# Broadcasting the tap weights over 128 rows of a cleared tile, with five constant matmuls ahead of it

## The chip, the cores and the metric

The kernel runs on one core of one Trainium2 chip. The time is the device time of one execution in microseconds (us). A core has a matrix engine (TensorE, PE in the profile, with its weight loads as PEld), a vector engine (VectorE, DVE), an activation engine (ScalarE, ACT), a general engine (GpSimd, POOL) and a queue engine (SyncE, SP). Loads and stores are DMA transfers, issued from the SP, ACT and POOL queues. Matmuls write to PSUM, from which ACT and VectorE bring the results to SBUF.

## The reference

The inputs are a sequence of 2048 tokens of width 640 and its weights, all bf16. Cut to what matters:

```python
h  = x + q_ln * (longconv(kv, ssm_k) + kv * ssm_D)   # q_ln = layernorm(x)
#   kv = (4-tap causal convolution of k along the sequence, with shift_k[d, 0..3]) * v
#   longconv: causal convolution over all 2048 tokens, by FFT in the reference
h2 = h + (silu(ln(h) @ w_gate) * (ln(h) @ w_up)) @ w_down   # inner width 1728
```

The tap weights `A_shift_k` (640 channels by 4 taps) are what the change concerns. Nothing of what is computed changes.

## The kernel before, in words

The sequence is cut into four blocks of 512 tokens (i = 0..3), and the long filter into four blocks as well (m = 0..3). Each block of kv and of the filter is taken by matmuls with tables of cosines and sines into 256 complex frequencies (`xf` and `kf`), the blocks are multiplied there (`p`), the sums are taken back by matmuls (`iv`), and the result goes through the second layer norm (`iv..m`, `s`, `v`, `r`, `n`) and a transposing load (`ht`) into the feed-forward part: `fg` (gate) and `fu` (up) matmuls, `sg`, `su` and `sv` on ACT, `mu` on VectorE, and `dn` (down), after which `rs` and `ra` add the residual and `out` stores. The order of the blocks is the string `SEQ`.

**Tasks and the plan.** Each step is a task, added with `g.add` under a name, with what it reads and writes. From this the class `_Graph` finds which task waits for which (`add`). The order on each engine is written out: `PLAN` holds for PE, ACT, DVE, POOL and SP a list of task numbers, and `arrange` takes them as they stand. `PLAN["units"]` says in which of four PSUM units each PSUM tile lies; a PE task that opens a tile waits for the readers of the tile that had the unit before. `emit` writes the waits and the instructions. An engine works strictly in its list's order, so a waiting task holds back all behind it. Since numbers are places in the order of `g.add`, one new task renumbers all after it.

**Fillers.** `PLAN["fills"]` names PE tasks ahead of which `filler` (L499) issues a number of matmuls of 128x512 on a tile of ones (`zmem`, a part of `gu`, set by POOL). They write into the PSUM tile that the task is about to open and their result is not used. Before, there are three ahead of `wb0` and one ahead of `k0t4.0`.

**The opening.** These are the tasks that the change touches, with their lines:

- `ident` and `wrow` (L466 and L469): loads of constants and of the tap weights. `wrow` is a tile of 5x64x4 elements by row. Of its rows only two are filled: row r holds the weights of channels 64r to 64r+63 of each of the five chunks of 128 channels. It goes out on the ACT queue; the other loads of the opening go out on SP.
- `wb0`, `wb4` (line L510): five matmuls that spread the two rows over the 128 partitions. The stationary operand `halfrow` (part of the constants `idall`) is 1 in row 0 for columns 0 to 63 and in row 1 for columns 64 to 127, else 0; the moving operand is one chunk of `wrow`, 256 columns. `wb0` has four chunks, `wb4` the last.
- `diag0`, `diag4` (L516): VectorE multiplies the spread weights with an identity, so that each tap is a diagonal 64x64 matrix per half of the partitions. All taps of all blocks use them.
- `k0t...` (L528): 20 transposes of the first block of K, and `k0e` (L455 on ACT, L457 on DVE): the copies into `kT0`.
- `tp0.4`, `tp0.2`, `tp0.0` (L731): the taps of block 0, 70 matmuls with 64 rows, two at a time in the two halves of the array.
- `kv0.c` (L749): VectorE multiplies the five chunks of the tap sums with v, out of PSUM.
- `kt0` (L547): transposes of the filter's block 0; `xf0` (L599): the forward transform of block 0; `la0` (L827 and after): the moments of x for the first layer norm.

Both operands of the broadcast are two rows high:

```python
last = e.matmul(pt.f(b // 2, 256, o=256 * (b % 2)), halfrow, wrow[0:2, c0 + b].rearrange("p x u -> p u x"), start=True, stop=True)
```

Of the kernel before, what the change touches and what calls it, by code (L numbers as in the profile page):

```python
# [12 lines left out]
P = 128  # L13
# [37 lines left out]
class _Graph:  # L51


    def __init__(self, nc, es):
        self.nc = nc
        self.es = es
        self.tasks = []
        self.tilelist = []
        self.lastw = {}
        self.readers = {}  # L60
        self.fills = PLAN.get("fills", {})
        self.ps = es.enter_context(nc.psum_tensor("ps", [P, 4096], dt.float32))
        self.psb = self.ps[:].bitcast(dt.bfloat16)
# [70 lines left out]
    def arrange(self, plan):  # L134
# [14 lines left out]
        byname = {t.name: t for t in self.tasks}  # L149
        for name, fill in self.fills.items():  # L150
            byname[name].deps.add(byname[fill[0]])
# [28 lines left out]
    def emit(self, block):  # L180
# [85 lines left out]
    "act":  # L266
# [10 lines left out]
    "dve":  # L277
# [10 lines left out]
    "pool":  # L288
        "19 17 15 16 125 165 174 158 192 183 223 225 224 342 396 362 281 371 285 401 380 289 406 389 343 293 420 415 527 466 "
        "470 561 474 552 478 579 570 684 586 591 529 705 710 698 637 732 723 641 645 750 649 741 "  # L290
        "",
    "sp":
        "0 2 3 8 4 6 10 7 230 9 11 13 14 235 296 226 12 229 297 227 481 231 167 176 228 234 295 233 194 185 482 232 364 282 373 "
# [5 lines left out]
        "01310112312301210312031012210230131023033303012010313012013"  # L299
        "",  # L300
    "fills": {
        "wb0": ["zmem", 3],
        "k0t4.0": ["zmem", 1],
    },
}
# [920 lines left out]
```

## Time and profile before

| what | us |
|---|---|
| median of the runs (258.29 to 261.71, three) | 258.99 |
| the profiled execution | 259.3 |
| its span, first to last instruction | 257.3 |
| PE busy | 249.3 |
| DVE busy | 200.0 |
| ACT busy | 184.5 |
| POOL busy | 58.5 |

The profile comes from one execution, and its times count from the start of the span. The 2.0 us between span and time lie around the program. In a timeline row stand the start, the duration, the engine, the line, the operation with the tile that it writes and those that it reads, how many were merged into the row, and in brackets the idle time of the engine before it and what ended it. Matmuls are pipelined: the duration of one is longer than the distance to the next. Buffer numbers are left out of the names, so that `kT` can be `kT0`, and `v` is `v0`. In a row of the windows stand the stretch, its length, then for PE and PEld the busy time and in brackets the number of instructions, then the granted TensorE clock, the DMA share and GB/s.

### The profile page before, as it was taken

What the parts mean: (1) busy time and instruction counts of PE and PEld (TensorE: products, weight loads), DVE (VectorE), ACT (ScalarE), POOL (GpSimd) and SP (SyncE); (2) the same over time, 40 slices, a digit from 0 to 9 for tenths busy, and PEclk for the clock granted to TensorE, in tenths of its full rate; (3) what the DMA queues carried; (4) which work ended last, traced back from release to release, by engine and by line L of the source; (5) the groups of instructions that cost most, each with busy time, mean ns of one, the idle gap of its engine ahead of it and who ended that gap; (6) DMA issues with size and microseconds to landing.
All of it is one profiled execution on the core that took longest, in us unless ns stands there. A gap on an engine that the chain in (4) does not pass through costs nothing.

```text
span 257.3 us, 5303 instructions
## 1 busy us (share of the span) xinstructions
PE 249.3 (97%) x2253; PEld 195.1 (76%) x2253; DVE 200.0 (78%) x256; ACT 184.5 (72%) x302; POOL 58.5 (23%) x56
## 2 busy tenths in 40 slices
PE   7999997999999999979999999999999999999995
PEld 4878773587888766868888866788886678888763
DVE  3689999999999998999999988999958524211242
ACT  2489999999996894577899789749981854516410
POOL 1001003082312052860030813333230314000000
PEclk9999999999999999999999999999999999999999
DMA  6998946788994058786946035497870152700011
GB/s 220 335 328 210 402 155 133 221 205 190 329 190 87 0 82 124 128 164 153 273 87 124 3 51 117 118 221 133 148 135 3 25 104 33 149 0 3 0 42 60
DMA packets 37620, 35.29 MB, mean 137 GB/s; under 512 B 21203, under 2 KB 32478, under 8 KB 37598
## 3 DMA queue, kind: packets, MB, share of 16 engines
q1 hardware_dynamic: 31792, 23.82, 33.2%
q0 software_dynamic: 5792, 11.14, 25.1%
q8 instruction: 17, 0.28, 0.5%
q14 instruction: 5, 0.04, 0.1%
q10 hardware_dynamic: 14, 0.01, 0.0%
HBM read 16.55 MB, written 2.62 MB: 75 GB/s over the span
## 4 chain that ended last, share of the span: by engine, by line
PE 62%; DVE 20%; ACT 11%; DMA 5%; issue 1%; SPq 0%; DVEq 0%
PE ps L1029 32%; PE ps L1115 16%; DVE tt L777 6%; PE ps L599 3%; DMA Y<-tt 3%; DVE Y L777 3%; PE ps L731 2%; ACT KO L455 2%; PE ps L919 2%; ACT C L455 2%; PE ps L581 2%; DVE C L777 2%; PE ps L992 2%; PE ps L619 2%; DMA k0n<-in_A_k_dram 1%; DVE gu L1050 1%
## 5 line engine op out<-in xcount | busy, mean ns | idle before, releaser
L1115 PE MATMUL ps<-Wd,gu 128*128 128x320 bf16 (+1 forms) x420 | 58.7, 300 | 0.0
L1115 PEld LDWEIGHTS ps<-Wd,gu 128*128 128x128 bf16 (+1 forms) x420 | 38.7, 97 | 18.4 <-issue 3.6
L777 DVE TENSOR_TENSOR tt<-XH,C 128x2560 bf16<-128x2560 bf16 (+1 forms) x31 | 47.8, 1571 | 1.5 <-DMA Y<-tt 0.9
L1050 DVE TENSOR_TENSOR gu<-gu,ub 128x1024 bf16<-128x1024 bf16 (+1 forms) x32 | 19.8, 620 | 26.2 <-ACT gu L1037 13.7
L1037 ACT ACTIVATE gu<-ps 128x1024 bf16<-128x1024 f32 (+1 forms) x32 | 29.4, 923 | 12.1 <-PE ps L1029 12.0
L1029 PE MATMUL ps<-hnT,GB 128*128 128x256 bf16 x280 | 34.0, 273 | 0.9 <-ACT XT L455 0.9
L1042 ACT ACTIVATE ub<-ps 128x1024 bf16<-128x1024 f32 x24 | 24.6, 1024 | 13.3 <-PE ps L1029 11.5
L1029 PE MATMUL ps<-hnT,UB 128*128 128x256 bf16 x280 | 33.8, 273 | 0.0
L1029 PEld LDWEIGHTS ps<-hnT,GB 128*128 128x128 bf16 x280 | 27.3, 98 | 4.3 <-ACT XT L455 1.0
L1029 PEld LDWEIGHTS ps<-hnT,UB 128*128 128x128 bf16 x280 | 27.3, 98 | 3.4 <-ACT KO L455 0.2
L1029 PE MATMUL ps<-hnT,GA 128*128 128x256 bf16 x240 | 28.8, 273 | 0.0
L1029 PE MATMUL ps<-hnT,UA 128*128 128x256 bf16 x240 | 28.5, 273 | 0.1
L837 POOL TENSOR_TENSOR mv<-mv,half 128x1 f32<-128x1 f32 x16 | 21.3, 1335 | 24.7 <-DVE mv L835 24.7
L1029 PEld LDWEIGHTS ps<-hnT,UA 128*128 128x128 bf16 x240 | 23.4, 98 | 3.4 <-ACT C L455 0.5
L1029 PEld LDWEIGHTS ps<-hnT,GA 128*128 128x128 bf16 x240 | 23.4, 98 | 3.2 <-DVE XH L458 0.3
L840 ACT ACTIVATE qo<-xh 128x640 bf16<-128x640 bf16 x28 | 21.0, 749 | 5.7 <-DMA xh<-in_A_q_dram 3.2
L581 PE MATMUL ps<-KT,tab 128*128 128x320 bf16 x128 | 19.6, 300 | 1.6 <-ACT K3r L455 0.7
L934 ACT ACTIVATE qo<-ps,one,st 128x640 bf16<-128x640 f32 x16 | 13.7, 886 | 9.8 <-PE ps L919 9.0
L568 POOL DMA_DIRECT2D xh<-RB x12 | 10.7, 888 | 34.7 <-DVE RB L1132 23.2
L581 PEld LDWEIGHTS ps<-KT,tab 128*128 128x128 bf16 x128 | 11.5, 98 | 8.2 <-ACT K3r L455 1.6
L837 POOL TENSOR_TENSOR st<-st,half 128x4 f32<-128x4 f32 x4 | 7.9, 1986 | 33.6 <-DVE st L832 21.8
L455 ACT ACTIVATE XH<-ps 128x640 bf16<-128x640 f32 x19 | 13.3, 736 | 1.5 <-PE ps L619 0.7
(112 smaller groups left out, 384.8 us busy)
## 6 DMA issues: line engine op xcount, KB each, us to landing
C<-US POOLq DMA_DIRECT2D x6, 640.0 KB, 5.9
kc<-in_A_ssm_k_dram SPq DMA_DIRECT2D x4, 640.0 KB, 10.6
xh<-in_A_q_dram SPq DMA_DIRECT2D x4, 640.0 KB, 5.5
out_dram<-xh SPq DMA_DIRECT2D x15, 160.0 KB, 2.0
kvo<-in_A_v_dram SPq DMA_DIRECT2D x3, 640.0 KB, 4.4
xh<-RB POOLq DMA_DIRECT2D x12, 160.0 KB, 3.0
Wd<-in_B_w_down_dram SPq DMA_DIRECT2D x1, 1280.0 KB, 7.8
C<-K3r POOLq DMA_DIRECT2D x2, 640.0 KB, 7.9
```

Source lines behind the costliest of these rows:

```text
L455: return e.activation(out=dst[1], in_=src(), func=ACTF.Copy, scale=scale)
L568: return g.add(name, "pool", lambda e, n: e.dma_start(dst, src, accum_op=ALU.add, max_dma_last_dim=4096), ("acc", 2 * int(np.prod(dst.shap ...
L581: last = e.matmul(pt.f(c, W), tab[:, f, cs, j], src[:, j, c * W:(c + 1) * W], start=(j == js[0]), stop=(j == js[1]))
L777: g.add(nm, "dve", lambda e, n_: e.tensor_tensor(out=d, in0=a, in1=b, op=op), ("sb", n * D), r=[a, b], w=[d])
L837: g.add(name + "r", "pool", lambda e, n: e.tensor_tensor(out=dst, in0=tmp, in1=hf, op=ALU.pow), ("pp", 4), r=[tmp, half[:]], w=[dst])
L840: g.add(name + "m", "act", lambda e, n: e.activation(out=junk, in_=x, func=ACTF.Identity, scale=-1.0 / D, accum_out=sm), ("aa", D, 0), r=[ ...
L934: g.add(nm + "e", "act", lambda e, n, pt=pt, q2=q2, s=s, j=j: e.activation(out=q2, in_=pt.f2(W), func=ACTF.Identity, scale=s[:, 3, j:j + 1 ...
L1029: last = e.matmul(pt.f(q // 2, 256, o=256 * (q % 2)), w[:, c, f0:f0 + P], hnT[:, c, cols], start=(c == 0), stop=(c == NC5 - 1))
L1037: g.add("sg%d.%d%d" % (i, h, gp), "act", lambda e, n, pa=pa, gv=gv, nf=nf: e.activation(out=gv, in_=pa.f(0, 256 * nf).rearrange("p (f x) - ...
L1042: g.add("su%d.%d%d" % (i, h, gp), "act", lambda e, n, pb=pb: e.activation(out=ub[:].rearrange("p b x -> p (b x)"), in_=pb.f(0, 1024), func ...
L1050: g.add("mu%d.%d%d" % (i, h, gp), "dve", lambda e, n, gv=gv, ubv=ubv: e.tensor_tensor(out=gv, in0=gv, in1=ubv, op=ALU.mult), ("sb", 256 * ...
L1115: last = e.matmul(pt.f(c, W), gu[k, fb, col(i, j)], Wd[k, fb, c * W:(c + 1) * W], start=st, stop=sp)
```

## The change

Three edits, and a plan with new numbers.

1. The whole tile `wrow` (128 rows) is set to zero by a new task `wz`, and the load of the two rows waits for that. In the plan `wz` is the first task of DVE. In the built program it is one instruction over 128x640 elements of four bytes.
2. `halfrow` and the moving operand of `wb0` and `wb4` have all 128 rows instead of two. The 126 further rows of `halfrow` are zeros from the constants, those of `wrow` are zeros from `wz`.
3. Five fillers stand ahead of `wb4`, which goes first; those ahead of `wb0` and `k0t4.0` are gone.

```diff
-        ident, id64, halfrow = idall[:, 0:P], idall[:, P:P + 64], idall[0:2, P + 64:P + 64 + P]
+        ident, id64, halfrow = idall[:, 0:P], idall[:, P:P + 64], idall[:, P + 64:P + 64 + P]
...
         load("ident", idall[:], id_d.ap(), 81920)
+        g.add("wz", "dve pool", lambda e, n: e.memset(wrow[:], 0.0), ("pm", 1280), w=[wrow[:]])
         load("wrow", wrow[0:2], A_shift_k.rearrange("(c r x) k -> r c x k", r=2, x=64), 20000, "act")
...
-                    last = e.matmul(pt.f(b // 2, 256, o=256 * (b % 2)), halfrow, wrow[0:2, c0 + b].rearrange("p x u -> p u x"), start=True, stop=True)
+                    last = e.matmul(pt.f(b // 2, 256, o=256 * (b % 2)), halfrow, wrow[:, c0 + b].rearrange("p x u -> p u x"), start=True, stop=True)
...
-            g.add("wb%d" % c0, "pe", mm, ("mm", 256, nc_), r=[halfrow, wrow[0:2]], pw=[pt])
+            g.add("wb%d" % c0, "pe", mm, ("mm", 256, nc_), r=[halfrow, wrow[:]], pw=[pt])
...
     "fills": {
-        "wb0": ["zmem", 3],
-        "k0t4.0": ["zmem", 1],
+        "wb4": ["zmem", 5],
     },
...
+        self.holds = PLAN.get("holds", {})
...
+        for name, k in self.holds.items():
+            self.order["dve"][byname[name + "v"].pos + k].deps.add(byname[name + "r"])
```

The plan has no `holds`, so the last lines do nothing here. All numbers in the lists go up by one behind the first, because of `wz`. Taken by name, the lists keep their order but for these tasks, each moved past a few neighbours:

- PE: `wb4` before `wb0`; `kt0.1` before `kt0.0`; `xf0.00` before `xf0.01`; `kt1.0` before `kt1.1`; `iv0.3` before `kf2.101` and `iv0.2`; `xf2.01` before `xf2.10`; `fu2.01` before `fg2.02`; `fu2.10` and then `fg2.03`, `fg2.10`, `fg2.11` in place of `fg2.03`, `fg2.11`, `fu2.10`, `fg2.10`; `fu3.02` before `fu3.01` and `fg3.01`; `fg3.10` before `fg3.11` and `dn3.0`; `fg3.13` before `fu3.12`.
- ACT: `drow` (a load) before `warm`, the first use of the table; `sg0.01` three places later; `gd1.0` before `la2.1x`; `la3.1x` goes to DVE; `la3.3m` before `sg2.10`; `gd2.0` comes from DVE, ahead of `sg2.13`; `su3.00` before `iv3.2s`.
- DVE: some twenty tasks swapped with a neighbour or two (products `p00`, `p23`, `p33`; `kb1.1` and `kv1.0`; `iv0.3g` before `iv0.1n`; `p01.c` and `xb1.0` two places earlier; `p02.c` before `iv1.0g`; `la2w`, `iv2.1v`, `la3.0x`, `la3.3x`, `lp3`), with `la3.1x` in and `gd2.0` out.
- POOL: `ra0.3` before `lp1`. SP: `x1` before `WdC`; `out2.1` three places earlier, before `ht3.3`, `out2.2` and `ht3.2`.

The PSUM units have new numbers throughout, and some thirty PE tasks open a unit that another task had before them than in the old plan.

More of the change, by code (lines that the diff above doesn't have):

```diff
@@ L257 @@
     "pe":
[7 rows of a table removed]
[7 rows of a table added]
         "",
     "act":
[9 rows of a table removed]
[9 rows of a table added]
         "",
     "dve":
[9 rows of a table removed]
[9 rows of a table added]
         "",
     "pool":
-        "19 17 15 16 125 165 174 158 192 183 223 225 224 342 396 362 281 371 285 401 380 289 406 389 343 293 420 415 527 466 "
-        "470 561 474 552 478 579 570 684 586 591 529 705 710 698 637 732 723 641 645 750 649 741 "
+        "20 18 16 17 126 166 175 159 193 184 224 226 225 343 397 363 282 372 286 402 381 290 407 390 294 344 421 416 528 467 "
+        "471 562 475 553 479 580 571 685 587 592 530 706 711 699 638 733 724 642 646 751 650 742 "
         "",
     "sp":
-        "0 2 3 8 4 6 10 7 230 9 11 13 14 235 296 226 12 229 297 227 481 231 167 176 228 234 295 233 194 185 482 232 364 282 373 "
-        "290 391 294 286 382 480 653 652 471 563 554 467 475 479 581 572 651 734 725 638 752 646 743 642 650 798 807 801 804 "
-        "810 "
+        "0 3 4 9 5 7 11 8 231 10 12 14 15 236 297 227 13 230 298 228 482 232 168 177 229 296 235 234 195 186 483 233 365 283 "
+        "374 291 392 295 287 383 481 654 653 472 564 555 468 476 480 582 573 652 735 726 639 643 753 647 744 651 799 808 802 "
+        "805 811 "
         "",
     "units":
-        "0131203132312001201201213230032110213023012230313133033220021021122013200230230222110332013110130232003210332301202110"
-        "01310112312301210312031012210230131023033303012010313012013"
+        "1030231230320110212032021013310223021302130021122321011020123103322031200210213000331220131330310213001320113103203230"
+        "02120223123012013210321310320310212032322230213202303021023"
         "",
     "fills": {
-        "wb0": ["zmem", 3],
-        "k0t4.0": ["zmem", 1],
+        "wb4": ["zmem", 5],
     },
```

50 rows, old and new, of the table PLAN are left out of this document.

## The prediction

> **What bounds the kernel now.** I read the page first, then the chain of waits, then the timeline of the first 20 us, since the changed instructions lie there, then the landings of the transfers, and last the rows around the places where the order changes. The page:
>
> ```profile
> span 257.3 us, 5303 instructions
> PE 249.3 (97%) x2253; PEld 195.1 (76%) x2253; DVE 200.0 (78%) x256; ACT 184.5 (72%) x302; POOL 58.5 (23%) x56
> PEclk9999999999999999999999999999999999999999
> PE 62%; DVE 20%; ACT 11%; DMA 5%; issue 1%; SPq 0%; DVEq 0%
> ```
>
> TensorE is busy for 97% of the span and carries 62% of the chain, so what is won or lost in one stage is handed to the end only if the stage lies on the chain. The chain at its beginning, with the same tap work much later as its last row:
>
> ```profile
> 1.14 3.47 DMA k0n<-in_A_k_dram
> ...
> 4.66 2.31 PE ps L528 x20
> 6.97 2.70 PE ps L731 x42
> ...
> 12.24 2.35 PE ps L599 x16
> ...
> 139.69 2.28 PE ps L731 x70
> ```
>
> So the opening is on the path: the load of K (k0n), 20 transposes, the first taps (tp0), the products kv0, and the first forward transform (xf0) at 12.24. The timeline of that stretch (start, duration, engine, line, tile, count, idle time before and its releaser):
>
> ```profile
> 0.72 0.52 POOL L497 MEMSET gu<- 128x512 bf16 x1 [0.29 <-POOLq L1211]
> ...
> 0.73 0.54 ACTq L447 DMA_DIRECT2D wrow<-in_A_shift_k_dram  x1
> ...
> 1.30 1.46 PE L502 MATMUL ps<-gu 128*128 128x512 bf16 x3 [1.30 <-POOL gu L497]
> ...
> 2.73 0.81 PEld L510 LDWEIGHTS ps<-wrow,idall 2*128 2x128 bf16 x5 [0.88 <-DMA wrow<-in_A_shift_k_dram]
> 2.76 1.29 PE L510 MATMUL ps<-wrow,idall 2*128 2x256 bf16 x5
> ...
> 3.99 0.61 PE L502 MATMUL ps<-gu 128*128 128x512 bf16 x1
> 4.09 1.55 DVE L516 TENSOR_TENSOR diag<-idall,ps 128x256 bf16<-128x256 bf16 x2 [4.09 <-PE ps L510]
> ...
> 5.94 0.69 DVE L457 COPY kT<-ps 128x512 bf16<-128x512 bf16 x1 [0.30 <-PE ps L528]
> ...
> 6.37 1.94 ACT L455 ACTIVATE kT<-ps 128x1024 bf16<-128x1024 bf16 x2 [3.56 <-PE ps L528]
> ...
> 6.90 3.80 PE L731 MATMUL ps<-diag,kT 64*128 64x256 bf16 x70
> ...
> 8.22 0.69 DVE L749 TENSOR_TENSOR kvo<-ps,v 128x512 bf16<-128x512 f32 x1 [1.58 <-DMA v<-in_A_v_dram]
> 9.70 2.48 DVE L749 TENSOR_TENSOR kvo<-ps,v 128x512 bf16<-128x512 f32 x4 [0.79 <-PE ps L731]
> 10.63 1.31 PE L547 MATMUL ps<-idall,kc 128*128 128x128 bf16 x20
> ...
> 13.36 1.40 DVE L827 BATCH_NORM_STATS2 bns<-xh 128x6 f32<-128x320 bf16 x3
> ...
> 18.63 1.25 PEld L547 LDWEIGHTS ps<-idall,kc 128*128 128x128 bf16 x20
> ```
>
> The same 70 taps take 3.80 us here and 2.28 at 139.69; 20 transposes take 2.31 at 4.66 and 1.31 at 10.63. TensorE therefore starts at a slower rate. The tap line by windows (matmuls that fall into each stretch) shows when that ends:
>
> ```profile
> 6.90:9.80 2.90, 2.90 (x46) 2.59 (x48) 1.00 1.01 308
> 9.80:10.70 0.90, 0.90 (x28) 0.76 (x24) 1.00 1.02 391
> ```
>
> 46 in 2.90 us are 16 a us, 28 in 0.90 are 31: the rate doubles at about 9.8. The granted clock stands at 1.00 in both rows and at 9 all along the page, so here that column does not show the slow start; the counts do. The array had work nearly all the way from 1.30 (three fillers, five two-row broadcasts, one filler, 20 transposes) without speeding up, and sped up after 2.9 us of taps. So either the two-row broadcasts or the transposes, or both, don't bring the fast rate on.
>
> **The change, part by part.** (1) The clearing, one instruction on VectorE over 128x640 four-byte elements, ahead of everything there, and the ACT queue holds the load of wrow until it is done. No row shows it. The nearest row is POOL's clearing above, 0.52 us for 512 elements: 0.52 x 640/512 = 0.65. The ends are two VectorE rows over 640 elements:
>
> ```profile
> 15.16 0.82 DVE L458 TENSOR_SCALAR KO<-ps 128x640 bf16<-128x640 f32 x1 [0.41 <-PE ps L581]
> ...
> 17.08 0.37 DVE L851 TENSOR_SCALAR xh<-xh,mvs 128x640 bf16<-128x640 bf16 x1
> ```
>
> I take 0.65, with 0.37 and 0.82 for the range; VectorE has nothing else before 4.09, so only the load feels it. Behind the waiting load on ACT stand drow, the table load and the warm-up; ACT's first real work is at 6.37, four us later, so they cost nothing. The load was issued at 0.73 and awaited until 2.73, two us at most; 0.65 later is 3.38. That is the value I take; the low end is 0.37 later (3.10), the high end is a transit like that of k0n on the chain, 3.47 us from an issue at 1.40, that is 4.87.
>
> (2) Five fillers. Three took 1.46 and a single one 0.61, so they follow one another at (1.46 - 0.61)/2 = 0.42. Five from 1.30 leave the array free at 3.40, when the load lands (3.38). They wait for the same POOL clearing as before and cost nothing; were the load earlier, they would hold the broadcasts up to 3.40. The single filler ahead of the transposes goes.
>
> (3) The broadcasts over 128 rows, five as before. The group's row has the time of one, 397 ns:
>
> ```profile
> L510 PE MATMUL ps<-wrow,idall 2*128 2x256 bf16 x5 | 1.3, 397 | 0.0
> ```
>
> Before, five took 1.29 with 0.40 for the last, so (1.29 - 0.40)/4 = 0.22 apart; other rows with 128 rows (fillers, 0.42 for 512 columns) have the same rate by column, so 0.22 holds. They run 3.40 to 4.69, and the array is free for the transposes at 3.40 + 5 x 0.22 = 4.50, before k0n lands at 4.61: no delay. wb4 now goes first, so diag4, the smaller, can start at 3.83 and is done before, and diag0 after wb0 at 4.72; the two took 1.55 together, and diag0 has four fifths of their elements, 1.24, hence ends at 5.96. The next on VectorE, the copy of kT, started at 5.94: cost 0.02, at most 0.1. This cover is thin: each us by which the load lands after 3.4 is a us on the copy, and on the first taps.
>
> (4) The rate. The stretch 1.30 to 4.69 is now filled with 3.2 us of 128-row matmuls (5 x 0.42 + 5 x 0.22), where 2.9 us of taps were enough before. I take it that the array is fast when the taps begin at 6.9. The bound on the other side is no effect: 0. What the fast rate is worth is read from what is late next. The first product of kv0 waits for v (the row at 8.22, 1.58 idle), not for the taps; the loads behind it are these:
>
> ```profile
> 3.05 0.53 SPq L447 DMA_DIRECT2D tab<-cst_tab  x1
> ...
> 3.62 0.48 SPq L447 DMA_DIRECT2D xh<-in_A_q_dram  x1
> ...
> 7.31 5.64 SPq L447 DMA_DIRECT2D kc<-in_A_ssm_k_dram  x3
> ```
>
> ```profile
> tab<-cst_tab SPq DMA_DIRECT2D x1, 256.0 KB, 7.8
> ...
> xh<-in_A_q_dram SPq DMA_DIRECT2D x1, 640.0 KB, 8.9
> ...
> kc<-in_A_ssm_k_dram SPq DMA_DIRECT2D x1, 640.0 KB, 10.2
> ```
>
> (The first fence has the issues, the second the us from issue to landing.) The product starts at 8.22 in either case, when v is there. What goes is the idle 0.79 behind it. At 2.28/70 = 0.033 a tap, 42 taps from 6.95 are through at 8.3 and the last 28, which wait for ACT's copies until 6.37 + 1.94 = 8.31, at 9.3; both are ahead of VectorE, which then needs 0.69 + 2.48 without a gap. xf0 starts at 12.24 - 0.79 = 11.45. Is anything else late by then? tab lands at 10.85; xh at 12.52, and the moments that need it move from 13.36 to 12.57; the first kc of the three at 7.31 + 10.2 = 17.5, and the transposes that need it from 18.63 to 17.84. All just fit; beyond 0.84 the load of xh would bind. So -0.79, bounds 0 and -0.84.
>
> (5) The order. PSUM units are renumbered, and some thirty tasks are moved past neighbours without a change of their own duration. Those with something to lose:
>
> ```profile
> 37.88 2.34 PE L924 MATMUL ps<-Y,itab 128*128 128x320 bf16 x16
> 40.43 0.87 ACT L934 ACTIVATE qo<-ps,one,st 128x640 bf16<-128x640 f32 x1
> ...
> 188.47 0.39 DVE L861 TENSOR_SCALAR xh<-xh,st 128x640 bf16<-128x640 bf16 x1 [0.91 <-ACT qo L842]
> ...
> 192.25 0.60 ACT L1037 ACTIVATE gu<-ps 128x512 bf16<-128x512 f32 x1 [0.56 <-PE ps L1029]
> ...
> 217.12 0.87 POOL L568 DMA_DIRECT2D xh<-RB  x1 [2.61 <-DVE RB L1132]
> ```
>
> iv0.3 goes ahead of kf2.101 and iv0.2, so iv0.2 ends about 1.1 us later (half of 2.34), near 40.2; ACT reads it at 40.43, so nothing, and up to 0.3 on ACT if that cover goes. la3.1x moves from ACT to VectorE (0.39) near 180, where the idle 0.91 at 188.47 takes it up; gd2.0 moves the other way, ahead of 0.56 of idle time on ACT. su3.00 passes iv3.2s, which holds that tile's normalisation back by 1 us, but its power on POOL is queued behind the issue at 217.12 anyway. On SP's queue x1 passes WdC, and out2.1 passes two transposing loads (ht3.3, ht3.2); all have us to spare. On POOL ra0.3 passes lp1, which only later residuals read. The swaps of gate, up and down matmuls in the last two blocks ask for the same operands in the same places, on an engine that never waits there. Sum: 0, with 0.3 either way.
>
> The sum: 0 + 0 + 0 - 0.79 + 0 = -0.8. The profiled execution took 259.3 (span 257.3); it would take 258.5. The median of the runs, 258.99, is 0.3 below that execution, so I put the time at 258.2.
>
> **The rivals.** First, no speed-up before the taps: the rate doubles near 9.8 again. For it: 5.6 us of mixed work did not bring it on, and the new broadcasts stream 126 cleared rows out of 128. Against it: 2.9 us of half-height taps did. All other terms are about 0, so 259.1. The page "TensorE: Matmul & The Clock Gate" of the Trainium skill, Part 1, bears on it: the clock goes up after a busy window of about 3.4 us, and the windows run freely, whatever the kernel does. By that rule a run of 3.2 us can't fill a window, and where the window must be quite full, the taps decide as before; the trace agrees so far that 2.9 us of taps, led by part of the transposes, came before the rise. The same page, Part 4, has transposes not count as busy in the same way, which no row here settles: either kind could be what did not count.
>
> Second, on the slower side: the load of wrow lands late, since it is now issued at 1.40 among the loads of k0n and v instead of ahead of them. At the high end, 4.87, the broadcasts run to 6.2, diag0 to 7.4, the copy of kT to 8.1, and the taps start 1.2 us after 6.90; that goes to the end: 260.2. It decides from a landing at about 3.6 on. Against it: it stands alone on the ACT queue, and before it took 2.0 at most.
>
> Third, the fast rate comes and its 0.8 us is given back: xh or kc lands later, or ACT's copies, not the taps, hold kv0. The moments have 0.05 to spare. Time 258.6 to 259.
>
> **How the numbers follow.** The forecast 0.57, no early rise 0.25, the late load 0.08, given back 0.10. The likeliest is 258.2. The runs of one kernel here reach from 258.29 to 261.71, 0.7 below the median and 2.7 above. Below I allow the forecast's spread and 0.3 of order, with 0.4 more for what I haven't seen: 256.8. Above, the second rival's 260.2 and 0.3: 260.5. The forecast's own range is 257.3 to 259.0. Over 2% is 5.2 us, about what a measurement of this kernel can tell from no change; the whole opening up to xf0 is 12 us and no case reaches it, so faster 0.01, same 0.97, slower 0.02, the last for a wait from the new order that I have missed.
>
> **What would show it.** Right: five fillers without a gap, broadcasts at about 3.4, the taps at 6.9 in about 2.3 to 2.6 us instead of 3.80, no idle time behind the first product, xf0 near 11.45, and everything later shifted by the same amount. Step (1) is wrong if the broadcasts wait for wrow beyond 3.6; (3) if diag0 ends after 6.1; (4) if the taps run at 16 a us; (5) if ACT waits at 40 or TensorE after 114. The prediction fails as a whole if xf0 starts after 12.3, or if it starts early and the chain loses it before 114.

## The result, and the profile after

| kernel | median, us | lowest to highest | runs |
|---|---|---|---|
| before | 258.62 | 257.75 to 261.85 | 22 |
| after | 259.34 | 257.93 to 260.25 | 22 |

The ratio of after to before is 1.0036, with a 95% interval from 1.0023 to 1.0048: the change costs 0.9 us, 0.6 to 1.2. Ratios and intervals are of the fast runs alone (those more than 1.5% over the fastest run of the same kernel are left out), so they differ a little from the ratio of the medians, which stand for all runs. The forecast was 258.2 us and a gain. The measured time lies inside the whole range that was given (256.8 to 260.5), outside the forecast's own (257.3 to 259.0), and on the other side of no change.

The profiled execution of after is no typical one. It took 257.93 us, the shortest of its 22, and its page looks better than that of before:

```profile
span 256.0 us, 5302 instructions
PE 247.7 (97%) x2254; PEld 193.8 (76%) x2254; DVE 201.0 (79%) x257; ACT 183.9 (72%) x302; POOL 55.9 (22%) x56
...
PE 62%; DVE 33%; POOL 2%; issue 1%; DMA 1%; ACT 0%; DVEq 0%
```

The last line is the chain that ended last. TensorE's share is what it was. VectorE's has gone from 20% to 33% and ScalarE's from 11% to 0%: the chain now runs through VectorE in places where it ran through ScalarE. POOL is new in it with 2%, and DMA has gone from 5% to 1%. The span is 1.3 us shorter than before's 257.3, though the medians go the other way by 0.7, so two traces alone can't say what the change did. Piece by piece the 1.3 us are these: xf0 starts at 11.31 instead of 12.24 (-0.93); a stretch on VectorE near 59 us is 0.49 longer; p02.c, a product placed ahead of iv1.0g, adds 0.12 near 88 us; and a wait for a DMA at 100 us is gone (-1.0). The sum is -1.3. The work below was to find out which of the four belong to the change. The opening of after in the timeline:

```profile
0.93 0.59 DVE L471 MEMSET wrow<- 128x640 uint32 x1 [0.93 <-PEq L1214]
...
1.30 2.31 PE L505 MATMUL ps<-gu 128*128 128x512 bf16 x5 [1.30 <-POOL gu L500]
...
1.55 0.55 ACTq L449 DMA_DIRECT2D wrow<-in_A_shift_k_dram  x1
...
3.95 1.30 PE L513 MATMUL ps<-wrow,idall 128*128 128x256 bf16 x5 [0.33 <-DMA wrow<-in_A_shift_k_dram]
...
5.29 1.22 DVE L519 TENSOR_TENSOR diag<-idall,ps 128x1024 bf16<-128x1024 bf16 x1 [0.49 <-PE ps L513]
...
6.43 0.68 DVE L459 COPY kT<-ps 128x512 bf16<-128x512 bf16 x1
...
7.17 2.47 PE L734 MATMUL ps<-diag,kT 64*128 64x256 bf16 x70 [0.40 <-DVE kT L459]
...
8.77 2.48 DVE L752 TENSOR_TENSOR kvo<-ps,v 128x512 bf16<-128x512 f32 x4 [0.20 <-PE ps L734]
...
11.31 2.35 PE L602 MATMUL ps<-kvo,tab 128*128 128x320 bf16 x16 [0.22 <-DVE kvo L752]
```

The clearing starts at 0.93, not at 0.73, and the load of wrow is issued at 1.55. The broadcasts start at 3.95, behind a wait for that load, instead of near 3.40. So diag0 ends at 6.51, the copy of kT starts 0.49 us later than in before, and the taps start at 7.17 instead of 6.90. But the 70 taps take 2.47 us instead of 3.80: TensorE is already fast.

### The profile page after: what moved, and what is told of

Read it like the earlier page. It is cut to its first block, busy times and chain, and to the rows that moved or that the text cites. A ratio compares the mean times of both kernels' runs of the same rounds, so it can differ in the third digit from the quotient of the medians.

```text
span 256.0 us, 5302 instructions
## 1 busy us (share of the span) xinstructions
PE 247.7 (97%) x2254; PEld 193.8 (76%) x2254; DVE 201.0 (79%) x257; ACT 183.9 (72%) x302; POOL 55.9 (22%) x56
## 4 chain that ended last, share of the span: by engine, by line
PE 62%; DVE 33%; POOL 2%; issue 1%; DMA 1%; ACT 0%; DVEq 0%
PE ps L1032 32%; PE ps L1118 16%; DVE tt L780 9%; DVE Y L780 6%; PE ps L602 3%; POOL mv L840 2%; PE ps L922 2%; PE ps L584 2%; DVE C L780 2%; DVE XH L637 2%; PE ps L995 2%; PE ps L622 2%; PE ps L734 2%; DVE gu L1053 1%; DVE OS L564 1%
## 5 line engine op out<-in xcount | busy, mean ns | idle before, releaser
L840 POOL TENSOR_TENSOR mv<-mv,half 128x1 f32<-128x1 f32 x16 | 18.4, 1154 | 27.7 <-DVE mv L838 27.7
```

Of the source, the lines that this page charges most:

```text
L840: g.add(name + "r", "pool", lambda e, n: e.tensor_tensor(out=dst, in0=tmp, in1=hf, op=ALU.pow), ("pp", 4), r=[tmp, half[:]], w=[dst])
```

## The experiments

Each kernel's time is given with its ratio to the kernel before on the same chip. In the diffs, the lists of `PLAN` are shown by the names of the tasks. A trace of such a kernel is called by the kernel's name. `v` on VectorE prepares the variance of a layer norm (one small instruction with one input, on `mv` or `st`), `r` on POOL takes its power (two inputs), and `n` on VectorE normalises with it. The tasks around them (`p`, `xb`, `kb`, `yb`, `mu` and `g`) are VectorE's products and sums of two inputs.

### The opening alone, and the order alone

The kernel after with the orders and units of before (only `wz`, the 128 rows, the fillers, `wb4` first and `drow` early are new), and the reverse:

```diff
 # opening_alone: against after
-    dve, pe, act, pool, sp, units: the new order
+    dve, pe, act, pool, sp, units: the order of before, with wz first, wb4 before wb0, drow before warm
 # order_alone: against before
-    dve, pe, act, pool, sp, units: the order of before
+    dve, pe, act, pool, sp, units: the new order, without wz, wb0 before wb4, warm before drow
```

> Only the opening of the change: the cleared tile, the 128-row broadcasts with wb4 first, five fillers, drow ahead of the warm-up; the order of all other tasks and the PSUM units as before the change. Theory A (the new order behind the opening costs 0.5 to 0.7 us, above all where VectorE waits for POOL's power of iv0.3, and the opening costs nothing on average): equal to the kernel before or up to 0.9 us faster. Rival B (the late landing of wrow costs, the order does not): 0.3 to 1.0 us slower than before, like the whole change. In the trace: taps in 2.3 to 2.6 us if the rate has risen before them, 3.8 if not; first forward transform at 11.3 to 11.5 or at 12.5.

> Only the new order and PSUM units; the opening as before the change (two-row broadcasts, three fillers and one, no clearing). Theory A: 0.5 to 0.9 us slower than before, with an idle gap of VectorE near 58 us ahead of iv0.3n. Rival B: equal to before within 0.2 us.

Measured: the opening alone 258.74 us, ratio 1.0007 (0.9984 to 1.003). The order alone 261.46, ratio 1.011 (1.0071 to 1.015). In this timing the loss goes with the order, not with the opening. The order alone is slower than the whole change; four of its six timed executions had a span of 259.3 us or more. One of the four is the traced one, and there the reason is the power la1r (below); the others left no trace.

### Is the time at which TensorE gets fast set by the program?

The two kernels as they are, for a second trace each:

> The kernel before as it is, for a second trace of its opening. If the time at which TensorE's rate doubles is an accident of the execution (theory A on the opening), it doubles at another time than 9.8 us, anywhere between 4 and 10, and where it falls before 7.5 the first element of the X transposes (xf0) starts near 11.3 instead of 12.24. If the rate is set by the program, it doubles at 9.8 again and xf0 starts at 12.2.

> The changed kernel as it is, for a second trace. If the moment of the doubling is an accident, it is another than 5.9 us; if it falls behind the first taps (7.2), xf0 starts near 12.2 as in the kernel before, instead of 11.3. If the clearing and the fillers set it, it stays within 0.3 us of 5.9. iv0.3r ends 7.2 us behind kb2.0 in both.

They took 258.43 and 262.91 us. The taps and xf0 in the timeline of before, second trace:

```profile
7.07 3.95 PE L731 MATMUL ps<-diag,kT 64*128 64x256 bf16 x70
...
12.41 1.80 PE L599 MATMUL ps<-kvo,tab 128*128 128x320 bf16 x12
```

(The last row ends at the window's edge, with 12 of the 16 matmuls.) After, second trace, with the broadcasts:

```profile
4.84 1.30 PE L513 MATMUL ps<-wrow,idall 128*128 128x256 bf16 x5 [1.22 <-DMA wrow<-in_A_shift_k_dram]
...
8.20 2.56 PE L734 MATMUL ps<-diag,kT 64*128 64x256 bf16 x70
...
12.43 1.80 PE L602 MATMUL ps<-kvo,tab 128*128 128x320 bf16 x12 [0.43 <-DVE kvo L752]
```

And the segment_alone kernel (below), which has the old opening:

```profile
6.91 2.72 PE L722 MATMUL ps<-diag,kT 64*128 64x256 bf16 x70
...
11.30 2.35 PE L590 MATMUL ps<-kvo,tab 128*128 128x320 bf16 x16 [0.31 <-DVE kvo L740]
```

The old opening has taps of 3.95 us in one execution and of 2.72 in another, and there xf0 starts at 11.30, as early as in after. The new opening has fast taps in both traces, but in the second wrow lands 0.9 us later and xf0 starts at 12.43. The moment at which the rate doubles can be read from the trace's records of the granted clock, which begin there; the windows count the time ahead of a record as 1.00. They begin at 9.8 and 10.3 us in the two traces of before, at 7.5 us in segment_alone and at 8.3 us in after's second trace. After's first trace and late_wrow (below) have no record; there the transposes go from 107 to 56 ns apart near 5.9 and 6.1 us. Over all traces of this case the rate doubles at 7.5 to 10.3 us with the old opening (six traces, mean 8.8) and at 4.1 to 9.8 with the new (fourteen, mean 6.9). In two of the fourteen it comes about as late as in before: 9.8 in segment_back's second trace and 9.2 in queues_new. So the rate rises earlier on average, but not in every execution.

The start of xf0 hardly moves: 11.25 to 12.41 us with the old opening (mean 11.82) and 11.31 to 12.77 with the new (mean 11.91). The first taps start at 6.92 and at 7.49 us on average, which takes back a part of the earlier rate. A second part is the load of v, which the first product of kv0 needs. It lands anywhere between 6.86 and 8.69 us, and in eleven of the twenty traces that product starts 0.1 us behind it. In late_wrow and vector_lists_back (below) the taps take 2.49 and 2.47 us, but v lands at 8.69 and 8.67, and xf0 starts at 11.93 and 11.91. On average v lands at 7.65 us with the old opening and at 8.07 with the new; with this scatter it is not shown that the change delays it.

Two more kernels varied the opening. First, after with two more fillers:

```diff
-        "wb4": ["zmem", 5],
+        "wb4": ["zmem", 7],
```

> The changed kernel with seven constant matmuls instead of five ahead of wb4, so that TensorE has no gap while wrow lands (3.41 to 3.95 in the trace after). They end near 4.26, so the broadcasts start 0.3 us later. If the gap keeps the rate from rising early in a good part of the executions, this is up to 0.5 us faster than the changed kernel; if the rate rises early anyway or does not depend on the gap, it is 0.2 to 0.3 us slower.

259.04 us, ratio 1.003 (1.0007 to 1.0052), xf0 at 11.56. Two fillers more change nothing that can be told from after. Second, the load of wrow was meant to land later still:

```diff
 # against opening_alone, act
-    wrow drow warm ...
+    drow warm wrow ...
```

> opening_alone with ScalarE's table load and warm ahead of the issue of wrow, which then lands some 0.8 us later still (near 4.9 us). Theory B' (the late landing costs, for it puts back the taps and moves the doubling of TensorE's rate): the first X transpose (xf0) starts 0.4 to 0.9 us later on average than the 11.75 and 11.99 of opening_alone, and the time is 0.4 to 0.9 us over opening_alone, 259.1 or more. Theory that the landing is hidden: 258.3 to 258.9, as opening_alone.

258.1 us, ratio 0.998 (0.9954 to 1.0005). The edit missed its aim: the trace has the issue of wrow at 1.55 again and the broadcasts at 3.88. It stands as another timing of the new opening; what a later landing costs was not tried.

### VectorE's stretch near 59 us

The chain of after has an entry that before's lacks, GpSimd's power iv0.3r (1.68 us from 57.02). First only iv0.3v was put back to its early place:

```diff
 # against after, dve
-    kb2.0 p01.c iv0.2g xb1.0 xb1.1 p01.d xb1.2 iv0.3v mu0.00 xb1.3 iv0.2v iv0.3n
+    kb2.0 p01.c iv0.2g iv0.3v xb1.0 xb1.1 p01.d xb1.2 mu0.00 xb1.3 iv0.2v iv0.3n
```

> The changed kernel with one VectorE task (iv0.3v, 0.1 us, which POOL's power waits for) put back ahead of xb1.0, four tasks earlier. Theory A: 0.4 to 0.6 us faster than the changed kernel, about equal to the kernel before; the gap of VectorE ahead of iv0.3n is gone. Rival B: no change, still 0.7 to 0.9 us slower than before.

259.06 us, ratio 1.003 (1.0003 to 1.0057): no help. The power starts 3.3 us earlier and still ends at the same place in the order. So the whole stretch (and `iv1.0g` ahead of `p02.c`) was put back in after, and put alone into before:

```diff
 # segment_back: against after, dve;  segment_alone: the reverse, against before
-    kb2.0 p01.c iv0.2g xb1.0 xb1.1 p01.d xb1.2 iv0.3v mu0.00 xb1.3 iv0.2v iv0.3n ... p02.c iv1.0g
+    kb2.0 iv0.2g xb1.1 iv0.3v p01.c xb1.0 p01.d xb1.2 mu0.00 iv0.2v xb1.3 iv0.3n ... iv1.0g p02.c
```

> The changed kernel in all but VectorE's list: the stretch kb2.0 to iv0.2n is back in the order of before, and iv1.0g stands ahead of p02.c again. Theory A (the cost of the change lies in this stretch: GpSimd's iv0.3r ends 7.2 us behind kb2.0 instead of 6.5, and VectorE loses 0.5 us at iv0.3n, 0.1 at p02.c): 258.6 to 258.8 us, 0.5 to 0.7 below the changed kernel's 259.3, a ratio to before of 0.999 to 1.001, and iv0.3r ends 6.5 us behind kb2.0. Rival B (the late landing of wrow costs, and the stretch doesn't): 259.3, a ratio of 1.003 to 1.004. Rival C (the rest of the order costs: TensorE's, ScalarE's, the queue's or the PSUM units): 259.2 or more, though iv0.3r ends 6.5 us behind kb2.0.

> The kernel before with that stretch of VectorE's list alone in the order of after (kb2.0 to iv0.2n, and p02.c ahead of iv1.0g). Theory A: 0.5 to 0.7 us over before, a ratio of 1.002 to 1.003, and iv0.3r ends 7.2 us behind kb2.0. Rivals B and C: no change, 0.999 to 1.001.

segment_alone: 258.65 us, ratio 1.0026 (1.0005 to 1.0046), as theory A has it. segment_back: 259.56, ratio 1.0041 (1.0019 to 1.0063), against it. In both traces the stretch itself behaves as expected: from the end of kb2.0 to that of iv0.3n it takes 7.23 us in segment_back and 7.72 in segment_alone. One pair was then swapped back in after:

```diff
 # against after, dve
-    mu0.00 xb1.3 iv0.2v iv0.3n
+    mu0.00 iv0.2v xb1.3 iv0.3n
```

> The changed kernel with one pair of VectorE's instructions back: iv0.2v (the one-input instruction on mv) ahead of xb1.3 instead of behind it. Theory D (GpSimd's two-input instruction iv0.3r is held while VectorE runs two-input instructions back to back, and gets through at the next one-input instruction): iv0.3r ends 6.5 us behind kb2.0's end instead of 7.2, and kb2.0's end to iv0.3n's end is 7.23 us instead of 7.72; 0.3 to 0.6 us below the changed kernel in time. Rival (it is another part of the stretch, such as p01.c ahead of iv0.2g): 7.2 and 7.72 stay.

259.11 us, ratio 1.0033 (0.9999 to 1.0067): the time is not below after's, where theory D has it 0.3 to 0.6 us lower, though in the trace the stretch takes 7.23 us, as theory D says. The timelines of VectorE and POOL, first before (kb2.0 is the first row, iv0.3v the row at 53.44, iv0.2v that at 58.38, iv0.3n the last; the two powers are one POOL row):

```profile
50.90 1.49 DVE L561 TENSOR_TENSOR C<-C,KO 128x2560 bf16<-128x2560 bf16 x1
...
53.44 0.15 DVE L835 TENSOR_SCALAR mv<-mv 128x1 f32<-128x1 f32 x1
...
53.68 5.98 POOL L837 TENSOR_TENSOR mv<-mv,half 128x1 f32<-128x1 f32 x2
...
58.38 0.15 DVE L835 TENSOR_SCALAR mv<-mv 128x1 f32<-128x1 f32 x1
58.44 0.81 DVE L634 TENSOR_TENSOR OS<-XH,OS 128x1280 bf16<-128x1280 bf16 x1
59.17 0.44 DVE L981 TENSOR_SCALAR qo<-xh,mv 128x640 bf16<-128x640 bf16 x1
```

After:

```profile
49.97 1.48 DVE L564 TENSOR_TENSOR C<-C,KO 128x2560 bf16<-128x2560 bf16 x1
...
56.79 0.15 DVE L838 TENSOR_SCALAR mv<-mv 128x1 f32<-128x1 f32 x1
56.85 0.68 DVE L1053 TENSOR_TENSOR gu<-gu,ub 128x1024 bf16<-128x1024 bf16 x1
57.02 2.19 POOL L840 TENSOR_TENSOR mv<-mv,half 128x1 f32<-128x1 f32 x2 [3.86 <-DVE mv L838]
57.45 0.82 DVE L637 TENSOR_TENSOR OS<-XH,OS 128x1280 bf16<-128x1280 bf16 x1
58.18 0.15 DVE L838 TENSOR_SCALAR mv<-mv 128x1 f32<-128x1 f32 x1
58.73 0.45 DVE L984 TENSOR_SCALAR qo<-xh,mv 128x640 bf16<-128x640 bf16 x1 [0.40 <-POOL mv L840]
```

The one swap back:

```profile
50.65 1.49 DVE L557 TENSOR_TENSOR C<-C,KO 128x2560 bf16<-128x2560 bf16 x1
...
57.70 1.71 POOL L833 TENSOR_TENSOR mv<-mv,half 128x1 f32<-128x1 f32 x2 [3.86 <-DVE mv L831]
58.12 0.15 DVE L831 TENSOR_SCALAR mv<-mv 128x1 f32<-128x1 f32 x1
58.19 0.82 DVE L630 TENSOR_TENSOR OS<-XH,OS 128x1280 bf16<-128x1280 bf16 x1
58.92 0.44 DVE L977 TENSOR_SCALAR qo<-xh,mv 128x640 bf16<-128x640 bf16 x1
```

In before the first of the two powers starts at 53.68 and lasts 5.21 us, to 58.89. The second takes 0.80. In after the first lasts 1.67, from 57.02 to 58.69. Whatever its start in these traces, it ends 0.36 us behind the end of iv0.2v, the one-input instruction on VectorE (58.53 in before, 58.33 in after); with the one swap back, where iv0.2v ends at 58.27, the power ends at 58.63. In power_early it starts at 53.72 and ends at 59.00, with iv0.2v ending at 58.64. Where xb1.3 stands ahead of iv0.2v, this release comes 0.73 us later, and VectorE, which would have been at iv0.3n 0.40 earlier, waits for it. That is the row with 0.40 and POOL as the releaser in after; before has no such wait. Of the 0.49 us that every trace of the new stretch loses, the swap returns all (7.23 us).

### Does VectorE hold GpSimd up?

The traces with the longest spans differ in another power, la1r, on the same engine. It takes 1.40 us in most traces and 10.68 in three (order_alone, after's second trace and segment_back's second). In before, la1v is followed by mu0.02; it was put one place later, so that the power begins beside the longer p11.1e:

```diff
 # against before, dve
-    p11.1c la1v mu0.02 p11.1e mu0.03
+    p11.1c mu0.02 la1v p11.1e mu0.03
```

> The kernel before with la1v one place later, behind mu0.02 instead of ahead of it, so that GpSimd's la1r starts beside the long two-input instruction p11.1e. Theory D: la1r is held until VectorE pauses, some 8 to 11 us instead of 1.40 in nearly every execution, and the time is 1.5 to 3 us over before. Rival (the 10.68 us seen in some executions have nothing to do with VectorE): la1r takes 1.40 us and the time stays within 0.3 us of before.

261.17 us, ratio 1.0093 (1.0067 to 1.0119): one swap of two short instructions costs 2.4 us. The power in before:

```profile
77.50 0.16 DVE L835 TENSOR_SCALAR st<-st 128x4 f32<-128x4 f32 x1
77.58 0.68 DVE L1050 TENSOR_TENSOR gu<-gu,ub 128x1024 bf16<-128x1024 bf16 x1
77.76 1.40 POOL L837 TENSOR_TENSOR st<-st,half 128x4 f32<-128x4 f32 x1 [1.72 <-DVE st L835]
...
78.18 1.48 DVE L777 TENSOR_TENSOR Y<-Y,tt 128x2560 bf16<-128x2560 bf16 x1
```

With the swap:

```profile
77.96 0.16 DVE L826 TENSOR_SCALAR st<-st 128x4 f32<-128x4 f32 x1
78.03 1.49 DVE L768 TENSOR_TENSOR Y<-Y,tt 128x2560 bf16<-128x2560 bf16 x1
78.22 10.08 POOL L828 TENSOR_TENSOR st<-st,half 128x4 f32<-128x4 f32 x1 [2.00 <-DVE st L826]
...
84.58 2.82 DVE L768 TENSOR_TENSOR Y<-XH,C 128x5120 bf16<-128x5120 bf16 x1
89.31 0.49 DVE L932 TENSOR_TENSOR xh<-xh,qo 128x640 bf16<-128x640 bf16 x1 [1.91 <-ACT qo L925]
```

The power ends at 88.30, 0.9 us behind the end of VectorE's row of two-input instructions at 87.40. VectorE then waits 1.91 us for ACT, which waits for the power. All ten timed executions took 260.27 us or more. So the hold-up is caused by what VectorE runs beside it.

The theory that GpSimd must wait for a one-input instruction or a pause doesn't fit every trace, though. In before, la1r ends at 79.16, 0.90 us behind the end of mu0.02 (78.26), and p11.1e, which has two inputs, follows mu0.02 at once (78.18). The same 0.90 us stand in all sixteen traces in which la1r takes 1.40 us. In the three others at the same place it went past that end and six more. In order_alone it got through behind p02.a (the row at 84.22), where the gap to the next two-input instruction is only 0.03 us:

```profile
77.26 10.68 POOL L828 TENSOR_TENSOR st<-st,half 128x4 f32<-128x4 f32 x1 [1.56 <-DVE st L826]
...
84.22 2.82 DVE L768 TENSOR_TENSOR Y<-XH,C 128x5120 bf16<-128x5120 bf16 x1
...
87.07 1.49 DVE L768 TENSOR_TENSOR Y<-Y 128x2560 bf16<-128x2560 bf16 x1
```

What decides at mu0.02 between 1.40 and 10.68 us is not shown.

### The rest of the order

segment_back was repeated beside after and opening_alone on one chip, and the rest of the order was put into before without the stretch (order_alone with the lines of segment_back):

> The changed kernel as it is, timed beside the next two on one chip. It serves as their measure: a ratio to before of 1.003 to 1.004 is expected, and a span 0.9 to 1.0 us over that of before.

> The same kernel as in segment_back (after with VectorE's stretch and iv1.0g in the order of before), beside after. Theory A (the stretch costs 0.6 us, whatever the rest): 0.4 to 0.7 us below after on the same chip. Rival C (the rest of the order costs as much, through waits that come in some executions only): level with after within 0.3 us, as in the first timing.

> The same kernel as in opening_alone, beside after. Theories A and C: 0.1 to 0.4 us over before, 0.6 or more below after. If the late landing of wrow costs (rival B): within 0.3 us of after.

> The opening of before with all of the new order and the new PSUM units, but VectorE's stretch kb2.0 to iv0.2n, and iv1.0g ahead of p02.c, as before. Theory A: within 0.3 us of before. Rival C: 0.7 us or more over before.

| kernel | median, us | ratio to before | interval |
|---|---|---|---|
| after | 258.89 | 1.0023 | 1.0001 to 1.0045 |
| segment_back | 259.36 | 1.005 | 1.0031 to 1.0069 |
| opening_alone | 258.88 | 1.0027 | 1.0004 to 1.0049 |
| order_without_segment | 258.07 | 1.002 | 0.9994 to 1.0046 |

segment_back misses theory A a second time. The opening alone comes out level with after here, as rival B has it, where its first timing (1.0007) had it level with before. So these timings don't settle whether the opening costs some 0.7 us or nothing. order_without_segment has the median of before on the same chip (258.10), as theory A has it, but its interval leaves room for up to 0.5%. Then the lists were put back engine by engine, each in the kernel after:

```diff
 # vector_lists_back: against after
-    dve, pool, sp: the new lists
+    dve, pool, sp: the lists of before (with wz; la3.1x and gd2.0 where after has them)
 # queues_new: against vector_lists_back
+    pool: ra0.3 before lp1;  sp: x1 before WdC, out2.1 before ht3.3
 # vector_rest_new: against segment_back
-    pool, sp: the new lists
+    pool, sp: the lists of before
```

> The changed kernel with the whole lists of VectorE, GpSimd and SyncE of before; the new opening, TensorE's and ScalarE's new order and the new PSUM units stay. Theory C (TensorE's, ScalarE's order or the units cost beside the new opening): 259.1 to 259.6, as segment_back. Theory A: 258.3 to 258.8, as opening_alone. In the trace, the stretches from kv0.0 to p12.0a would show which of them is longer than in opening_alone.

> vector_lists_back with the new lists of GpSimd and SyncE put back in (ra0.3 ahead of lp1, x1 ahead of WdC, out2.1 ahead of ht3.3); VectorE's list stays that of before. Theory E (the part of the cost that segment_back doesn't remove comes from these transfers, through waits for DMAs): 259.0 or more, a ratio of 1.003 to 1.005. Theory F (it comes from VectorE's other moves): 0.998 to 1.001, as vector_lists_back.

> segment_back with the lists of GpSimd and SyncE of before: of the new order on these engines only VectorE's moves outside the stretch kb2.0 to iv0.2n are left. Theory E: 0.998 to 1.001. Theory F: 1.003 to 1.005, as segment_back, and traces in which a GpSimd instruction takes longer (iv1.1r 1.47 us instead of 0.73, or la1r 10.68 instead of 1.40).

vector_lists_back: 258.53 us, ratio 0.9991 (0.9967 to 1.0015). As theory A has it, nothing can be seen here of a cost of TensorE's and ScalarE's orders, the PSUM units or the opening. queues_new: 258.58, 1.0017 (0.9991 to 1.0042), between theories E and F. vector_rest_new: 258.49, 1.001 (0.9991 to 1.0029), as theory E has it. Neither alone shows the 0.4 to 0.5% of segment_back. No kernel of the study can be told from before on the faster side.

The traces say more than these times. Up to p13.1a, near 123 us, most stretches of VectorE's work take the same time to 0.02 us in all of them, and behind it every trace but one (seven_fillers, 134.8) needs another 134.0 to 134.2. From p12.0a to p13.1a it is 21.7 us, but 22.2 in after's second trace and 22.6 in order_alone. What differs lies in a few places (in us, between the ends of the named tasks on VectorE):

| trace | xf0 starts | kb2.0 to iv0.3n | yb1.1 to p12.0a | span |
|---|---|---|---|---|
| before | 12.24 | 7.23 | 18.15 | 257.3 |
| before, second | 12.41 | 7.23 | 17.15 | 256.5 |
| opening_alone | 11.75 | 7.23 | 17.57 | 256.2 |
| vector_lists_back | 11.91 | 7.23 | 17.49 | 256.3 |
| segment_alone | 11.30 | 7.72 | 17.28 | 255.9 |
| after | 11.31 | 7.72 | 17.27 | 256.0 |
| after, second | 12.43 | 7.72 | 20.31 | 260.8 |
| power_early | 11.61 | 7.73 | 17.83 | 256.8 |
| one_swap_back | 11.99 | 7.23 | 17.29 | 256.2 |
| segment_back | 11.44 | 7.23 | 17.96 | 257.1 |
| segment_back, second | 12.77 | 7.23 | 19.26 | 259.0 |

The third column is set by the swap. The fourth has a floor of 17.15, and 0.12 more where p02.c stands ahead of iv1.0g. What lies above is a wait of that execution: for a DMA in before, for la1r in the two rows over 19, for iv1.1r in power_early and, in part, in segment_back. In the waits of before it is

```profile
DVE tt L777 <- DMA Y<-tt: 0.9, 1, 0.9
```

and it is gone in before's second trace, so it isn't the change that removed it. Two traces have waits of TensorE elsewhere. In the waits of segment_back, between 12 and 17 us, it is one for the table of the transforms:

```profile
PE ps L577 <- DMA tab<-cst_tab: 0.6, 1, 0.6
```

In those of seven_fillers, near 209 us, it is one for a transposing load:

```profile
PE ps L1025 <- DMA hnT<-qo: 0.6, 1, 0.6
```

In the timeline of queues_new the power iv1.1r takes 1.47 us, and iv1.1n ends 0.55 later behind yb1.1 than in before:

```profile
98.04 1.47 POOL L833 TENSOR_TENSOR mv<-mv,half 128x1 f32<-128x1 f32 x1 [1.19 <-DVE mv L831]
```

In that of after the same power takes 0.73:

```profile
97.44 0.73 POOL L840 TENSOR_TENSOR mv<-mv,half 128x1 f32<-128x1 f32 x1 [1.18 <-DVE mv L838]
```

Of the eleven traces with GpSimd's and SyncE's new lists, three have iv1.1r at 1.47 (power_early, segment_back, queues_new) and three others have la1r at 10.68. Of the eight with the lists of before, leaving out the one made to have it, none has either. That speaks for the new queues bringing such hold-ups on more often, but how they do so is not shown, and queues_new alone doesn't show it in time.

## Why the prediction was wrong

Step (1) took 0.65 us for the clearing and a landing of wrow at 3.38. The clearing took 0.59. But it began at 0.93, and the load, issued at 1.55, was awaited until 3.95 in the first trace, 2.4 us behind its issue, where the step took two and kept more for the high end. The start of the broadcasts lay between 3.84 and 4.84 in the fourteen traces. This is the second rival's mechanism, with its place right.

Step (2) was right: the five fillers ran from 1.30 without holding anything up.

Step (3) was right in its durations (diag0 1.22 us against 1.24), and wrong in its end: 6.51 instead of 5.96, since it started from step (1).

Step (4) had the mechanism right and its worth wrong. The rate did rise before the taps in after's first trace, and xf0 started at 11.31 against 11.45. What failed is the base: the step took the 0.79 us from a trace of before in which the rate happened to double at 9.8 us. Kernels with the old opening start xf0 at 11.25 and 11.30 in other executions. The step also took it that the first product starts at 8.22 "in either case", with v; v landed between 6.86 and 8.69. That xf0 came within 0.14 us of the forecast in after's first trace was luck. Averaged over the traces the opening gains nothing (11.82 and 11.91), and opening_alone, late_wrow and vector_lists_back lie at 1.0007, 0.998 and 0.9991, though the second timing of the opening has 1.0027. The Trainium skill's rule in "TensorE: Matmul & The Clock Gate", Part 1, that the windows run freely and the warm-up therefore varies from run to run, stood in the prediction beside the first rival; the traces agree, with taps of 3.95 and 2.72 us behind the same opening, and it should have been put against the base as well.

Step (5), "Sum: 0, with 0.3 either way", failed, and as far as is known it carries the sign. Two places cost 0.49 and 0.12 us, 0.61 in all, in every trace that has them: the pair xb1.3 and iv0.2v, and p02.c ahead of iv1.0g. Put alone into before they cost time as well (segment_alone, 1.0026). Neither was in the step's list. It looked for tasks that are late for the next engine, and took it that a short instruction may move past its neighbour for free. It didn't ask which GpSimd instruction was running meanwhile. The rest of the step was right where it could be tested: TensorE's and ScalarE's moves and the units show no cost (vector_lists_back, 0.9991).

The 0.61 us are two thirds of the 0.93 us of the first timing and as much as the 0.6 of the second, but that they are the change's cost is not shown. What stays open is why kernels with these two places put back don't get faster: the one swap 1.0033, segment_back 1.0041 and 1.005, where their traces lack the 0.49 us. The waits listed above come in some executions only, and one trace each doesn't tell how often. That the queues of GpSimd and SyncE make them more frequent is the best guess, not a finding.

None of the three rivals had the right reason. The first, no early rise, did come, in two of the fourteen traces of the new opening. The second came nearest in the opening, but its 260.2 was not paid at the end. The third's loss behind the opening did come, at places that it didn't name: the load of v, and the order near 59 us.

## What to carry to other kernels

Before pricing a gain at the start of a kernel from one trace, ask whether the same program would start so in the next execution. One more trace would not have been enough here (12.24 and 12.41 us for xf0 in the two of before); the six traces of the old opening have 1.16 us of scatter. When a plan is reordered, look at which engine runs beside the moved instruction, not only at who waits for its result: here the place of a 0.15 us instruction decided when another engine got through. Where a trace of after and the medians disagree, cut the trace into stretches between tasks and compare them with several traces, so that what repeats is separated from what doesn't.

## What the runs showed of the hardware

GpSimd's power with two inputs can be held up by a row of two-input instructions on VectorE, over many of them (5.21 us, 10.68 and 10.08). It then gets through behind a one-input instruction (iv0.2v) or a gap between two rows (1.91 us in power_at_long_op, 0.03 us in order_alone). The same instruction at the same place takes 1.40 or 10.68 us, with nothing in between in nineteen traces; where it takes 1.40, it gets through between two two-input instructions without a gap. So that turn is not ruled out, but it was missed at six and seven ends in a row. The page "SBUF — State Buffer" of the Trainium skill, section "Who interferes with whom", has it that a VectorE instruction with two SBUF inputs and a GpSimd instruction that reads SBUF exclude each other, and that the first to be issued wins. The traces agree so far that the power's end keeps a fixed distance from the end of an instruction of VectorE: 0.36 us from that of iv0.2v for 128x1 elements (before, after, power_early and one_swap_back), 0.90 us for 128x4 (la1r, in all twenty). They add that after the end of one such instruction the next one of VectorE can go first, many times over.

When TensorE idles behind such a hold-up it can lose its rate. It waited 3.1 us for ACT in order_alone and 3.3 in after's second trace, and the granted clock fell; it waited 2.7 us in power_at_long_op and in segment_back's second trace, and the clock stayed at 1.00. In order_alone the windows 80 to 90 us and 90 to 100 us show a granted clock of 0.97 and 0.86:

```profile
80.00:90.00 10.00, 6.93 (x57) 5.35 (x55) 9.58 (x9) 4.26 (x6) 7.94 (x1) 0.97 0.01 2
90.00:100.00 10.00, 10.00 (x66) 6.37 (x65) 7.40 (x13) 8.36 (x17) 2.97 (x3) 0.86 0.50 78
```

TensorE was busy for 6.93 of the first 10 us. In the second window it was busy all the time, with 66 matmuls. The same window in before has 76:

```profile
90.00:100.00 10.00, 10.00 (x76) 6.74 (x76) 8.69 (x14) 7.02 (x15) 4.38 (x4) 1.00 0.74 92
```
